# Attention sinks of the last batch moved into the preceding key block, with late fetches for the displaced keys

## The chip, the core and the metric

The kernel runs on one core of a Trainium2 chip. The metric is the device time of one execution in microseconds (us). Six executions of the kernel before took 226.69 to 228.21 us, median 227.55.

## What is computed

Attention with a sliding window and four sinks, then layer normalisation and a two-layer product with a residual:

```python
keep = is_sink | in_window          # first 4 keys, or 0 <= q - k < 128
scores = np.where(keep, scale * q @ k.T, -1e9)
a = exp(scores - max); a = a / a.sum(-1)
x = a @ v                           # 4 batches, 8 heads, 768 rows, head width 64
xn = (x - mu) / sqrt(var + 1e-6) * g_ln
out = x + relu(xn @ w_ch1) @ w_ch2  # 512 -> 2048 -> 512
```

Inputs and output are fp32. The products are made in bf16.

## The kernel before, in words

The 4 x 768 rows are cut into 24 blocks of 128 rows, six to a batch (`b, r = divmod(t, 6)`). A block sees its own keys and those of the block ahead of it. For r = 0 and 1 that holds the sinks as well. For r >= 2 the four sink keys of the batch get products of their own.

For each block: load q, k and v (lines 267, 272 and 275, on the GpSimd queue, POOL); transpose q and k (on PE for the first eight blocks, line 347; by DMA from the sync queue SP for the others, line 369); scores `ps` (line 406, PE) and, for r >= 2, sink scores `pk` (line 413, PE); exponentials on ACT (lines 435 and 482); masks on the vector engine DVE (line 444); the products with the values into `po` (sinks at line 496, own and preceding keys at lines 501 and 504, PE); normalisation with row sums (lines 514 and 517, DVE); centring (lines 526 and 529, DVE); variance (lines 537 and 538, DVE); transpose of the centred block `xc` to `xnt` (line 559 on PE for the first eight blocks, line 565 by DMA from SP for the others).

The sink keys of a batch are copied once from its first block into `ks` (line 454, DVE). The sink values are spread over partitions by two small products `pv` (line 466, PE) and masked (line 472, DVE) into `vs`.

Four blocks make a group, so there are six groups. `m1` multiplies a group by w_ch1 in 16 steps (line 603, PE), each followed by a relu on ACT or DVE (lines 619 and 617). `m2` multiplies by w_ch2, four steps for each block (line 638, PE), followed by the output step on DVE (line 650) and a store on SP (line 659). One step of either is four matmuls of 512 columns. The inverse deviation of a group is a power on POOL (line 548), fed by a small DVE step (line 546); it shares POOL's queue with the loads.

The order on every engine's queue is made when the program is built. `Planner` (lines 15 to 126) places tasks one by one: the task whose inputs, buffers and engine are free first, by costs and delays written next to each task, then by a priority. The engines themselves run their queues strictly in order and wait on semaphores. Scores of later blocks are held back by a pace: block t waits for step 8(t-4)-16 of the products (lines 698 to 701). Buffers are rings with a number of slots each (`RINGS`, line 166): `pa` are four PSUM banks, `xn` the `xnt` buffers, `h1` the buffers after the relu, `qk` the transposed q and k. In the opening, PE is given filler matmuls (`warm`, line 181, and `w0`, line 314), as many as the planned gap in time has room for.

Of the kernel before, what the change touches and what calls it, by code (L numbers as in the profile page):

```python
# [7 lines left out]
FP32 = mybir.dt.float32  # L8
BF16 = mybir.dt.bfloat16
I32 = mybir.dt.int32  # L10
# [4 lines left out]
class Planner:  # L15
# [16 lines left out]
    def run(self, free, warm_until):  # L32
# [14 lines left out]
        ends = {}  # L47
        dma_free = free["DMA"]
        order = []
        queued = []  # L50
        while ready:
# [37 lines left out]
            if e == "PE":  # L89
                gaps[i] = start - free[e] if start < warm_until else 0.0  # L90
            free[e] = start + cost
            end = start + cost + (self.LAG[e] if t["lag"] is None else t["lag"])
            ends[i] = start + cost
            if t["land"] is not None:
                dma_free = max(dma_free, start + 1.5) + t["land"]
                end = dma_free + (0.6 if t["lag"] is None else t["lag"])
                if t["desc"]:
                    queued.append((dma_free, t["desc"]))
            done[i] = (e if t["land"] is None else None, start + cost, end)
# [13 lines left out]

    @staticmethod
    def room(queued, desc, ring=4096):

        for at, d in reversed(queued):
            desc += d
            if desc > ring:
                return at  # L120
        return 0.0

    def emit(self, order):
        for i, e, slots in order:
            self.gap = self.gaps.get(i, 0.0)
            self.tasks[i]["emit"](e, *slots)
# [3 lines left out]
def kernel(  # L130
# [34 lines left out]
    LDN, QKN = 4, 5  # L165
    RINGS = dict(pa=4, ps=2, ld=LDN, qk=QKN, ks=2, vs=2, e=8, es=3, xc=4, xn=4, h1=32, ot=4)
    plan = Planner(RINGS)
# [13 lines left out]
    def warm(bank_):  # L181

        for _ in range(int(plan.gap * WARM / .056)):
            nc.tensor.matmul(bank_, lhsT=ident, rhs=ident, start=True, stop=True, skip_group_check=True)
# [20 lines left out]
    blk_h = consts.tile([128, 4], BF16, name="blk_h")  # L205
    ks_t = [consts.tile([128, 2, 4, 32], BF16, name=f"ks_{i}") for i in range(2)]
    xt = [consts.tile([128, DM], BF16, name=f"xt_{t}") for t in range(NT)]

# [9 lines left out]
    def make_masks():  # L218
        v_ = nc.vector
        nc.gpsimd.iota(iota_d, pattern=[[1, 128]], base=0, channel_multiplier=-1)  # L220
        nc.gpsimd.iota(iota_h, pattern=[[-32, 4]], base=0, channel_multiplier=1)
        v_.tensor_scalar(ident, iota_d, 0.0, None, op0=ALU.is_equal)
        v_.tensor_scalar(mask_std[:, 0:128], iota_d, 0.0, None, op0=ALU.is_ge)
        v_.tensor_scalar(tmp_h, iota_h, float(NS), None, op0=ALU.is_lt)
        v_.tensor_tensor(mask_zero, mask_std[:, 0:128],
                         tmp_h[:, 0:1].to_broadcast([128, 128]), op=ALU.max)
        v_.tensor_scalar(neg_zero, mask_zero, 1.0, 30000.0, op0=ALU.subtract, op1=ALU.mult)
# [22 lines left out]
    d_q, d_k, d_v = {}, {}, {}  # L250
    last_load = [None]

    def load(fn, land, take=(), desc=1024):
        i = plan.add({"POOL": 0.88}, [], fn, (0,), take=take, land=land, after=last_load[0], desc=desc)
        last_load[0] = i
        return i
# [55 lines left out]

    P = {}
    def w0(e, s):
        b_ = bank(s, "pw")
        for _ in range(WARM0):
            nc.tensor.matmul(b_[:, 0:128], lhsT=zeros, rhs=zeros, start=True, stop=True, skip_group_check=True)
# [3 lines left out]
    def opening():  # L321
        plan.add({"PE": .1}, [], w0, (0, -1, 0), take=[("pa", "w0", 0)])
        D["mb"] = plan.add({"DVE": .45}, [d_q[0]], make_masks_b, (0, 0, 1))
        D["mc"] = plan.add({"DVE": 1.3}, [d_q[0]], make_masks_c, (0, 1, 5))


# [3 lines left out]
    def block(t):  # L330
# [3 lines left out]
        last = r == RB - 1  # L334
        split = t in SPLIT


# [18 lines left out]
        n_s = lambda u: 2 if u in SPLIT_S else 1  # L356
        qk_readers = n_s(t) + (0 if last else n_s(t + 1)) + (1 if r == 0 else 0)
        if split:
# [26 lines left out]
        def sc(halves):  # L385
# [30 lines left out]
            return f  # L416

        s_ = []
        for halves in (((0,), (1,)) if t in SPLIT_S else ((0, 1),)):
            cost = .22 * nkb + .43 * nkb * (t in MPE)  # L420
            sink = r >= 2 and halves[-1] == 1
            x_ = plan.add({"PE": cost * len(halves) / 2 + .15 + SINK * sink},
                          d_c[t] + (d_c[t - 1] if r else []) + ([D["mb"]] if t in MPE and r else [])
                          + ([d_ks[b]] if sink else []), sc(halves),
                          (0, t, 2), take=[("ps", ("ps", t, h), 1) for h in halves]
                          + ([("pa", ("pk", t), 1), ("es", ("es", t), 2)] if sink else []),
                          drop=[("qk", t)] + ([("qk", t - 1)] if r else []) + ([("ks", b)] if sink else []))
            s_ += [x_] * len(halves)
# [3 lines left out]
        for half in range(2):  # L432
            def ex(e, s, half=half):
                E[t, half] = buf("e", s, [128, 2, 2, 2, 128], BF16, "e")
                nc.scalar.activation(E[t, half][:, :, :, 0:nkb, :], P["ps", t, half][:, :, :, 0:nkb, :], AF.Exp, scale=scale)  # L435

            x_ = plan.add({"ACT": 1.02 if r else .59}, [s_[half]], ex, (0, t, 3),
                          take=[("e", ("e", t, half), 1)], drop=[("ps", t, half)])

            def mk(e, half=half):  # L440
                m = (mask_zero, mask_one)[r] if r < 2 else mask_std
                w = 128 * nkb
                ee = E[t, half].rearrange("p a b c d -> p (a b) (c d)")
                nc.vector.tensor_mul(ee[:, :, 0:w], ee[:, :, 0:w], m[:, 0:w].unsqueeze(1).to_broadcast([128, 4, w]))  # L444

            ms.append(x_ if t in MPE else plan.add({"DVE": .68 if r else .4}, [x_], mk, (0, t, 4)))


        if r == 0:
            def mks(e, s):  # L450
                ks_of[b] = ks_t[s]
                for h2 in range(2):
                    rows = slice(64 * h2, 64 * h2 + 64)
                    nc.vector.tensor_copy(ks_of[b][rows, h2], qkT[t][rows, 1, :, 0:32])

            d_ks[b] = plan.add({"DVE": .3}, d_c[t], mks, (0, t + 2, 0), take=[("ks", ("ks", b), 4)],
                               drop=[("qk", t)])
            vs_d = []
            for half in range(2):
                hs = slice(4 * half, 4 * half + 4)  # L460

                def pv_(e, s, *s2, half=half, hs=hs):
                    if s2:
# [4 lines left out]
                pv = plan.add({"PE": .13}, [d_v[t], D["mc"], s_[0]] + vs_d, pv_, (0, t + 2, 0),  # L468
                              take=[("pa", ("pv", b, half), 1)] + ([("vs", ("vs", b), 8)] if half == 0 else []))

# [7 lines left out]

        a_deps = [d_v[t]] + ([d_v[t - 1]] if r else [])
        if r >= 2:  # L480
            def es_(e):
# [6 lines left out]
        for half in range(2):  # L488
            def av(e, s, half=half):
# [3 lines left out]
                ee = E[t, half]  # L493
                if r >= 2:
                    for h2 in range(2):
# [3 lines left out]
                for hh in range(4):  # L499
                    h = 4 * half + hh  # L500
                    nc.tensor.matmul(po[:, hh, :], lhsT=ee[:, h % 2, hh // 2, 0, :], rhs=vn[:, t, h, :],  # L501
                                     start=(r < 2 and hh == 0), stop=(r == 0), skip_group_check=True)
                    if r > 0:
                        nc.tensor.matmul(po[:, hh, :], lhsT=ee[:, h % 2, hh // 2, 1, :], rhs=vn[:, t - 1, h, :],  # L504
                                         start=False, stop=True, skip_group_check=True)

            a = plan.add({"PE": (.12, .25, .37)[min(r, 2)]}, a_deps + [ms[half]], av, (0, t, 5),
                         take=[("pa", ("po", t, half), 1)],
                         drop=[("e", t, half)] + ([("es", t), ("vs", b)] if r >= 2 else []))

            def nm(e, half=half):
                po = P["po", t, half]
                rc = small.tile([128, 4], FP32, name="rc")
                nc.vector.reciprocal(rc, po[:, :, 64])  # L514
# [6 lines left out]

            ns.append(plan.add({"DVE": .60}, [a], nm, (0, t, 6), drop=[("po", t, half)]))

# [9 lines left out]
        def st(e):  # L533
            if ti == 0:
                mvg[g] = small.tile([128, 4, 2], FP32, name="mvg")
            st_ = small.tile([128, 6], FP32, name="st")
            nc.vector.bn_stats(st_, xt[t])  # L537
            nc.vector.bn_aggr(mvg[g][:, ti, :], st_)

        v_ = d_var[t] = plan.add({"DVE": .87}, [l_] + ([d_var[t - 1]] if ti else []), st, (0, t + 6, 7))  # L540
        if ti == len(GROUPS[g]) - 1:
# [40 lines left out]
    quanta = []  # L582
    ks_of = {}


    h1 = {}
# [86 lines left out]
    MPE = set(range(4))  # L673
    W2AT = 6
    SEQ = [x for g in range(NG) for x in ((1, g), (2, g))]
    for t, parts in ((0, "qk"), (1, "qk"), (0, "v"), (2, "qk"), (1, "v"), (3, "qk"), (2, "v"), (3, "v")):
# [14 lines left out]
    for i, (layer, g) in enumerate(SEQ):  # L691
        mark[layer, g] = len(quanta)
        (m1(g, i, SUBS.get(g)) if layer == 1 else m2(g, i))
    pace = []
    for layer, g in SEQ:
# [6 lines left out]
    make_consts()  # L702
    order = plan.run(dict(PE=3.5, DVE=4.6, ACT=2.0, POOL=1.2, SP=1.0, DMA=3.4), WARM_UNTIL)
    plan.emit(order)
# [35 lines left out]
```

## Time and profile before

| | |
|---|---|
| median of six executions | 227.55 us (226.69 to 228.21) |
| the profiled execution | 228.21 us |
| its span in the profile | 226.1 us |
| PE busy | 216.8 us, 96% of the span |
| DVE busy | 134.7 us, 60% |
| ACT busy | 104.1 us, 46% |
| POOL busy | 76.0 us, 34% |
| chain that ended last: PE, DMA, POOL, DVE | 81%, 7%, 5%, 4% |
| granted TensorE clock, mean | 1.00 |

The profile shows one execution. Its page gives busy times, 40 slices of the span (each digit the busy share in tenths), the chain of work that ended last, followed back from the end, and groups of instructions with count, busy time, mean duration, and the idle time ahead of them with what ended it. In the chain in order of time, a line holds the start in us, the length in us, and what ran. A matmul's record lasts longer than its share of PE's time, since matmuls overlap; the chain's pieces show the share. `DMA qkT<-qkn` is a transfer on the chain, from its issue to its landing.

### The profile page before, as it was taken

To read this page: it belongs to the slowest core of one execution; us is meant where nothing else is said; L and a number is where in the kernel's file an instruction comes from. 1 tells how busy PE (TensorE), PEld (TensorE's weight loads), DVE (VectorE), ACT (ScalarE), POOL (GpSimd) and SP (SyncE) were. 2 spreads that over 40 slices of the span, in tenths; PEclk is the share of its full clock that TensorE was granted. 3 is DMA by queue.
4 is the path that set the end of the run, shared out by engine and by line. 5 is a ranking of instruction groups with operands and counts; after the bars stand their busy time and mean duration, and the time that the engine had idled before them with its cause. 6 is when DMAs were issued, how large, how long until landed. Compare 5 with 4: busy or idle time off the path is not lost.

```text
span 226.1 us, 4819 instructions
## 1 busy us (share of the span) xinstructions
PE 216.8 (96%) x1938; PEld 121.9 (54%) x1964; DVE 134.7 (60%) x399; ACT 104.1 (46%) x166; POOL 76.0 (34%) x92
## 2 busy tenths in 40 slices
PE   8998999999799999999999999999999999999993
PEld 7665887655355554554555544554554544444452
DVE  5776988779567989755658673845863722100121
ACT  2486888344168650356660347641266610267000
POOL 7994365592593440950269000010000010000000
PEclk9999999999999999999999999999999999999999
DMA  6999999999999999999999996213121011200112
GB/s 42 142 157 202 183 184 207 168 176 185 152 188 143 147 140 196 153 159 169 138 105 163 140 202 120 47 26 116 49 70 23 3 43 73 93 0 3 46 46 93
DMA packets 108853, 26.52 MB, mean 117 GB/s; under 512 B 101536, under 2 KB 105888, under 8 KB 108832
## 3 DMA queue, kind: packets, MB, share of 16 engines
q0 software_dynamic: 79104, 13.64, 80.3%
q1 hardware_dynamic: 29728, 12.59, 31.7%
q8 instruction: 15, 0.25, 0.5%
q14 instruction: 6, 0.05, 0.1%
HBM read 27.27 MB, written 6.29 MB: 148 GB/s over the span
## 4 chain that ended last, share of the span: by engine, by line
PE 81%; DMA 7%; POOL 5%; DVE 4%; issue 1%; ACT 0%; POOLq 0%; ACTq 0%
PE ph L603 34%; PE pc L638 34%; PE ps L406 5%; DMA qkT<-qkn 4%; DMA w1s<-in_moe_w_ch_dram 3%; PE po L501 2%; PE po L504 2%; POOL qkn L267 2%; POOL qkn L272 2%; PE po L496 2%; POOL vn L275 2%; PE pk L413 1%; DVE w1s L299 1%; PE pt L347 1%; DVE xt L517 1%
## 5 line engine op out<-in xcount | busy, mean ns | idle before, releaser
L603 PE MATMUL ph<-xnt,w1s 128*128 128x512 bf16 (+1 forms) x434 | 88.9, 348 | 1.3 <-DVE w1s L299 0.3
L638 PE MATMUL pc<-w2s,h 128*128 128x512 bf16 (+1 forms) x388 | 87.1, 370 | 1.0 <-issue 0.5
L619 ACT ACTIVATE h<-ph 128x512 bf16<-128x512 f32 (+1 forms) x84 | 45.9, 547 | 53.7 <-PE ph L603 52.0
L603 PEld LDWEIGHTS <-w1s 128*128 128x128 bf16 x448 | 41.5, 98 | 35.7 <-DVE w1s L299 0.9
L638 PEld LDWEIGHTS <-h 128*128 128x128 bf16 x400 | 37.4, 98 | 37.8
L435 ACT ACTIVATE e<-ps 128x1024 bf16<-128x1024 f32 (+1 forms) x48 | 43.7, 954 | 12.9 <-PE ps L406 12.9
L650 DVE SCALAR_TENSOR_TENSOR ot<-pc,rsg,xt 128x512 f32<-128x512 f32 (+1 forms) x25 | 18.2, 726 | 38.4 <-PE pc L638 38.4
L548 POOL TENSOR_TENSOR rsg<-ve,eps_half 128x4 f32<-128x4 f32 x6 | 6.2, 1028 | 79.6 <-DVE ve L546 79.6
L267 POOL DMA_DIRECT2D qkn<-in_q_dram x24 | 21.9, 915 | 18.4 <-DMA qkT<-qkn 15.7
L444 DVE TENSOR_TENSOR e<-e,mask_std 128x1024 bf16<-128x1024 bf16 x28 | 18.9, 684 | 10.9 <-ACT e L435 10.9
L617 DVE TENSOR_SCALAR h<-ph 128x512 bf16<-128x512 f32 (+1 forms) x28 | 15.9, 570 | 14.9 <-PE ph L603 14.9
L272 POOL DMA_DIRECT2D qkn<-in_k_dram x24 | 21.8, 909 | 3.1 <-DMA w1s<-in_moe_w_ch_dram 1.6
L275 POOL DMA_DIRECT2D vn<-in_v_dram x24 | 21.9, 915 | 1.7 <-DMA w1s<-in_moe_w_ch_dram 1.7
L517 DVE SCALAR_TENSOR_TENSOR xt<-po,rc 128x256 bf16<-128x256 f32 x48 | 20.4, 425 | 1.7
L501 PE MATMUL po<-vn,e 128*128 128x65 bf16 x192 | 17.1, 193 | 0.3 <-DMA vn<-in_v_dram 0.3
L537 DVE BATCH_NORM_STATS2 st<-xt 128x6 f32<-128x512 bf16 x24 | 16.4, 685 | 0.0
L406 PE MATMUL ps<-qkT 64*128 64x128 bf16 x352 | 14.7, 218 | 1.6 <-DMA qkT<-qkn 1.3
L406 PEld LDWEIGHTS <-qkT 64*128 64x128 bf16 x352 | 9.9, 94 | 11.3 <-issue 8.1
L482 ACT ACTIVATE es<-pk 128x256 bf16<-128x256 f32 x16 | 6.1, 384 | 20.7 <-PE pk L413 20.7
L501 PEld LDWEIGHTS <-e 128*128 128x128 bf16 x192 | 14.0, 97 | 2.5 <-issue 0.4
L514 DVE RECIPROCAL rc<-po 128x4 f32<-128x4 f32 x48 | 8.6, 178 | 11.4 <-PE po L504 10.3
L504 PE MATMUL po<-vn,e 128*128 128x65 bf16 x160 | 14.9, 193 | 0.0
(66 smaller groups left out, 144.1 us busy)
## 6 DMA issues: line engine op xcount, KB each, us to landing
out_dram<-ot SPq DMA_DIRECT2D x23, 256.0 KB, 3.6
qkn<-in_q_dram POOLq DMA_DIRECT2D x24, 128.0 KB, 7.1
qkn<-in_k_dram POOLq DMA_DIRECT2D x24, 128.0 KB, 7.2
vn<-in_v_dram POOLq DMA_DIRECT2D x24, 128.0 KB, 7.9
w1s<-in_moe_w_ch_dram POOLq DMA_DIRECT2D x4, 512.0 KB, 10.5
w2s<-in_moe_w_ch_dram POOLq DMA_DIRECT2D x4, 512.0 KB, 11.8
qkT<-qkn SPq DMA_TRANSPOSE x16, 7.7
xnt<-xc SPq DMA_TRANSPOSE x16, 5.2
```

Of the source, the lines that this page charges most:

```text
L267: nc.gpsimd.dma_start(qn[t][:, 0], q[b, :, rows, :].rearrange("h p d -> p h d"))
L272: nc.gpsimd.dma_start(qn[t][:, 1], k[b, :, rows, :].rearrange("h p d -> p h d"))
L275: nc.gpsimd.dma_start(vn[:, t, :, 0:64], v[b, :, rows, :].rearrange("h p d -> p h d"))
L406: nc.tensor.matmul(ps[:, h2, hh, kb, :], lhsT=qkT[t - kb][rows, 1, hp, :], rhs=qkT[t][rows, 0, hp, :], start=(hh == 0 and kb == 0 and t no ...
L435: nc.scalar.activation(E[t, half][:, :, :, 0:nkb, :], P["ps", t, half][:, :, :, 0:nkb, :], AF.Exp, scale=scale)
L444: nc.vector.tensor_mul(ee[:, :, 0:w], ee[:, :, 0:w], m[:, 0:w].unsqueeze(1).to_broadcast([128, 4, w]))
L501: nc.tensor.matmul(po[:, hh, :], lhsT=ee[:, h % 2, hh // 2, 0, :], rhs=vn[:, t, h, :], start=(r < 2 and hh == 0), stop=(r == 0), skip_grou ...
L504: nc.tensor.matmul(po[:, hh, :], lhsT=ee[:, h % 2, hh // 2, 1, :], rhs=vn[:, t - 1, h, :], start=False, stop=True, skip_group_check=True)
L517: nc.vector.scalar_tensor_tensor(xt[t][:, 256 * half:256 * half + 256].rearrange("p (h d) -> p h d", h=4), in0=po[:, :, 0:64], scalar=1.0, ...
L603: nc.tensor.matmul(ph, lhsT=w1s[:, j, 128 * ht:128 * (ht + 1)], rhs=xnt[g][:, j, cols], start=(j == 0), stop=(j == NDM - 1))
L619: nc.scalar.activation(o, i, AF.Relu)
L638: nc.tensor.matmul(P["pc", t, cols.start][:, cols], lhsT=h1[g, ht][:, 128 * ti:128 * (ti + 1)], rhs=w2s[:, ht, cols], start=(ht == 0), sto ...
```

## The change

In blocks with r >= 2 of the last batch (`FOLD = 18`: blocks 20 to 23), the sink keys and values are written over rows 0 to 3 of the preceding block (`fold_k`, `fold_v`, DVE), after that block's own use of them. The mask of r = 1, which lets those rows through, is taken for these blocks. `pk`, its exponential, the two sink products of `po` and `pv` are left out there. The overwritten rows 1 to 3 still belong to the window of the block's first three query rows. Their part is computed apart: nine small fetches on SP bring the three queries, keys and values of each of the four blocks to 12 partitions, a chain of 13 DVE steps and one exponential makes the weighted sums, a small DMA spreads them to three partitions, and the normalisation adds them to rows 0 to 2 of `po`. The fetches wait for a memset that waits for product step 112, the first `m1` step of group 3.

The variance may be computed on ACT as well, with a scaled square and its row sum. The ring of `xnt` buffers shrinks from 4 to 2, that of `h1` from 32 to 20. A number of planned costs and delays differ (loads, the opening, the normalisation), and the planned landing of transfers from SP takes the loads under way on POOL into account. The filler matmuls ahead of a planned 7 us count as 0.11 us each and no longer as 0.056. The built program has 32 `pk` matmuls fewer (96), 16 sink products of `po` fewer (48), two `pv` fewer (6), and 54 filler matmuls by `warm` for 66. On ACT stand ten of the 24 variances.

```diff
+    FOLD = 18
-    RINGS = dict(pa=4, ps=2, ld=LDN, qk=QKN, ks=2, vs=2, e=8, es=3, xc=4, xn=4, h1=32, ot=4)
+    RINGS = dict(pa=4, ps=2, ld=LDN, qk=QKN, ks=2, kss=2, vs=2, e=8, es=3, xc=4, xn=2, h1=20, ot=4)
...
-        for _ in range(int(plan.gap * WARM / .056)):
+        for _ in range(int(plan.gap * WARM / (.056 if plan.at > 7.0 else .11))):
...
+        nc.gpsimd.iota(iota_c, pattern=[[4, 3]], base=4, channel_multiplier=-1)
...
+    def corrections(gate):
+        def hold(e):
+            nc.vector.memset(f_in[:, 0, :, 0:1], 0.0)
+            nc.vector.tensor_scalar(mask_c[:, 0, :], iota_c, 0.0, None, op0=ALU.is_gt)
+        h_ = plan.add({"DVE": .3}, [gate], hold, (0, 7, 7))
...
+                def fetch(e, n=n, b=b, i=i):
+                    to = f_in[12 * n + 4 * i:12 * n + 4 * i + 4]
+                    nc.sync.dma_start(to[:, :, 0, :], q[b, :, 256:768, :].rearrange("h (r x) d -> x r h d", x=128)[i])
+                    for at, src in ((1, k), (4, v)):
+                        nc.sync.dma_start(to[:, :, at:at + 3, :].rearrange("r h p d -> r h (p d)"),
...
+        for p in range(3):
+            d = step(.68, fetched + [d] if p else fetched, lambda e, p=p: nc.vector.tensor_mul(fk[:, :, p, :], fk[:, :, p, :], fq))
+            d = step(.65, [d], lambda e, p=p: nc.vector.tensor_reduce(
+                fs[:, :, p:p + 1], fk[:, :, p:p + 1, :], axis=mybir.AxisListType.X, op=ALU.add))
+        d = step(.3, [d], lambda e: nc.scalar.activation(fe, fs, AF.Exp, scale=scale), "ACT")
+        d = step(.2, [d], lambda e: nc.vector.tensor_mul(fe, fe, mask_c.to_broadcast([FR, H, 3])))
+        for p in range(3):
+            d = step(.65, [d], lambda e, p=p: nc.vector.tensor_mul(
+                fv[:, :, p, :], fv[:, :, p, :], fe[:, :, p:p + 1].to_broadcast([FR, H, 64])))
+        d = step(.2, [d], lambda e: nc.vector.tensor_reduce(fc[:, :, 64:65], fe.unsqueeze(2),
+                                                            axis=mybir.AxisListType.X, op=ALU.add))
+        d = step(.65, [d], lambda e: nc.vector.tensor_add(fv[:, :, 0, :], fv[:, :, 0, :], fv[:, :, 1, :]))
+        d = step(.65, [d], lambda e: nc.vector.tensor_add(fc[:, :, 0:64], fv[:, :, 0, :], fv[:, :, 2, :]))
+        def spread(e):
+            for n in range(len(FB)):
+                nc.sync.dma_start(fcb[:, 4 * n:4 * n + 4], fc[12 * n:12 * n + 12])
...
+        if fold:
+            def fold_k(e):
+                nc.vector.tensor_copy(qkT[t - 1][:, 1, :, 0:4], kss_of[b])
+            def fold_v(e):
+                nc.vector.tensor_copy(vn[0:4, t - 1], vn[0:4, t - r])
...
-            sink = r >= 2 and halves[-1] == 1
+            sink = r >= 2 and not fold and halves[-1] == 1
...
+                if fold:
+                    nc.vector.tensor_add(po[0:3], po[0:3], fcb[:, 4 * FB.index(b) + r - 2, 4 * half:4 * half + 4, :])
...
+                root = 1.0 / float(DM) ** 0.5
+                st_ = small.tile([128, 1], FP32, name="nb")
+                nc.scalar.mul(st_, sums[t][:, 2:3], -root)
+                nc.scalar.activation(junk, xt[t], AF.Square, bias=st_, scale=root, accum_out=mvg[g][:, ti, 1:2])
...
-        v_ = d_var[t] = plan.add({"DVE": .87}, [l_] + ([d_var[t - 1]] if ti else []), st, (0, t + 6, 7))
+        v_ = d_var[t] = plan.add({"DVE": .87, "ACT": 1.1}, [l_] + ([d_var[t - 1]] if ti else []), st, (0, t + 6, 7))
...
-    order = plan.run(dict(PE=3.5, DVE=4.6, ACT=2.0, POOL=1.2, SP=1.0, DMA=3.4), WARM_UNTIL)
+    order = plan.run(dict(PE=1.0, DVE=4.6, ACT=2.0, POOL=1.2, SP=1.0, DMA=3.4), WARM_UNTIL)
```

## The prediction, made before the run

> **What bounds the kernel now.** I read the page first (busy shares, the 40 slices, the chain), then the windows, then the chain in order of time, then the rows of the vector, scalar, GpSimd and sync engines where the change touches them.
>
> ```profile
> PE 216.8 (96%) x1938; PEld 121.9 (54%) x1964; DVE 134.7 (60%) x399; ACT 104.1 (46%) x166; POOL 76.0 (34%) x92
> PE   8998999999799999999999999999999999999993
> DVE  5776988779567989755658673845863722100121
> DMA  6999999999999999999999996213121011200112
> PE 81%; DMA 7%; POOL 5%; DVE 4%; issue 1%; ACT 0%; POOLq 0%; ACTq 0%
> ```
>
> PE is busy 216.8 of 226.1 us and carries 81% of the chain. The slices show two regimes: up to slice 24 (about 136 us) the DMA engines are also at 9 tenths, after it they are nearly idle. So early work can be held by data, late work only by PE or by what feeds it. The one large wait of PE on data is at 61 us:
>
> ```profile
> 51.09 0.35 PE ps L406 x8
> ...
> 52.16 8.71 DMA qkT<-qkn
> ...
> 60.92 0.62 PE ps L406 x16
> ```
>
> The scores of block 8 need a transpose that was issued at 52.16 and landed 8.71 us later; PE stood idle 1.33 us before them. From there to 210 us PE idles some 1.3 us in all (the windows), in pieces of 0.05 to 0.25. So what is saved behind 61 us is paid out in full; what is saved ahead of it first has to bring that landing forward.
>
> ```profile
> 132.34 0.22 PE pv L466
> ...
> 147.88 0.55 PE ps L406 x16
> 148.43 0.23 PE pk L413 x8
> 148.66 0.16 issue
> ...
> 151.35 0.12 PE po L496 x2
> ```
>
> These are rows of the last batch: sink scores (pk), sink values (po L496) and the gather of sink values (pv, two matmuls) all lie on the chain.
>
> **What the change removes from PE.** Its blocks 20 to 23 lose pk: 0.23, 0.23, 0.22 and 0.23 us on the chain (at 148.43, 156.94, 165.44, 173.95), together 0.91. They lose two L496 pairs each, 8 x 0.12 = 0.96. The batch loses both pv, 0.22. Sum 2.09 us, all behind 61 us. The built order of instructions confirms the counts (pk 128 to 96, L496 64 to 48, pv 8 to 6). Product matmuls and window matmuls are as many as before.
>
> **What it adds to the vector queue (DVE), and what hides it.** The correction of three query rows per block is 11 long instructions (12 partitions, 512 fp32 elements: three products, three sums, three weightings, two additions) and two short ones. No row shows fp32 from SBUF on 12 partitions; these are the nearest:
>
> ```profile
> L444 DVE TENSOR_TENSOR e<-e,mask_std 128x1024 bf16<-128x1024 bf16 x28 | 18.9, 684 | 10.9 <-ACT e L435 10.9
> L650 DVE SCALAR_TENSOR_TENSOR ot<-pc,rsg,xt 128x512 f32<-128x512 f32 x23 | 17.2, 747 | 36.2 <-PE pc L638 36.2
> L537 DVE BATCH_NORM_STATS2 st<-xt 128x6 f32<-128x512 bf16 x24 | 16.4, 685 | 0.0
> ```
>
> L650 has the same width in fp32. Back to back it costs 0.66 (it starts at 151.57, the next at 152.23). I take 0.66 for the long ones; below, 0.43 (the 512-wide bf16 rows); above, 1.05, as no row shows a sum over 64. So 11 x 0.66 + 2 x 0.2 = 7.7 us, and 0.4 for the small exponential on ACT in the middle. In the new order it starts behind the first normalisation of block 19 (ends 143.93 before). Then come that block's second normalisation 0.56, the output step 0.66, the centring 0.51, the copy of sink values 0.35 (0.4 at most, by the 512-wide copy), and block 20's masks 2 x 0.61: 3.3. The masks are ready at 143.9 + 7.7 + 0.4 + 3.3 = 155.3. PE now asks for them ten product steps after block 20's scores: 148.4 + 10 x 0.865 = 157.1. Slack 1.8 us: no cost in the likeliest case.
>
> Behind that each folded normalisation grows by an addition on three partitions, 260 wide: 0.34, the pace of the 260-wide L472 row. It becomes 0.9. Two copies of sinks per block (about 0.2 and 0.35) replace nothing, and four variance steps (0.9 each) move to ACT. Laid out by these paces, block 21's masks come 0.3 us ahead of PE, block 22's 0.4, block 23's about level. I put 0.2 us of waits there (0 to 1.0).
>
> ```profile
> 140.00:150.00 10.00, 9.79 (x91) 5.01 (x88) 4.64 (x14) 7.13 (x12) 1.03 (x1) 1.00 0.21 41
> 150.00:160.00 10.00, 9.95 (x91) 5.13 (x90) 6.51 (x16) 3.15 (x5) 0.00 (x0) 1.00 0.21 66
> 160.00:168.40 8.40, 8.29 (x77) 4.23 (x76) 5.79 (x16) 2.82 (x4) 0.00 (x0) 1.00 0.28 80
> ```
>
> In each window the busy times stand in the order PE, PEld, DVE, ACT, POOL. DVE was at 46 to 69% and rises to over 80%; ACT has room for the variance, a 512-wide activation of about 0.6 and a small one, four times, less four es of 0.38 that go.
>
> **Queues that the nine fetches pass.** They stand on SP behind the transpose of block 22 (132.41, held until block 18's scores) and one store. The memset ahead of them waits for the first step of group 3 on PE, 132.0; DVE has nothing ready then but that step's own output. Nine issues at 0.33 to 0.53 (store rows) end by 139.5; with 2.2 us to landing (stores' median) they are there at 141.7, and DVE asks at 143.9. Behind them on SP wait the transposes xnt of block 18 (needed at 164) and qkT of block 23 (140.42 anyway, held by block 19's scores). The small store of the corrections goes out at about 152.5, and delays the transpose of block 19 to 154; at 5.2 us to landing it beats 162. Zero, with 2 to 4 us of cover each.
>
> **Buffers.** Group product buffers 32 to 20 and xnt buffers 4 to 2: a group's first product already stands behind the last product of the group before on PE; zero. Variance on ACT in earlier batches: off the chain; zero.
>
> **The opening.** One more iota on POOL between the first two loads: 0.08 (the gap that iota_h takes, 2.59 to 2.67). The loads never run dry from there on, so I count 0.1 on the landing at 61. Other reordering around 20 us lets PE do block 2's output transpose and half of block 3 while w1s is scaled; before, PE waited there (0.32, 0.22, 0.20 and part of a 1.16 us row that holds 0.43 of work). That lead of 0.3 to 1.0 us should be lost again at 61 us: the keys of block 8 were issued only at 44.28, when a w2s piece landed, and take 7.2. I count nothing.
>
> The Trainium skill speaks against one edit here. TensorE: Matmul & The Clock Gate, Part 1, says the array runs at half rate until some 3.4 us of activity and falls back after an idle window as long; the change cuts filler matmuls ahead of 8 us from 36 to 11. The row: the first 34 take 3.81 us, 112 ns each, later ones 56, while the granted clock reads 1.00 throughout. By the rule a fallback would double about 1.6 us of work; but the gaps opened are some 0.9, 0.4 and 0.4 us, short of its window, and fillers and idle time ahead of 20 us cover 1.6. Zero.
>
> **POOL's order** changes where it matters to DMA:
>
> ```profile
> 58.91 1.03 POOL L548 TENSOR_TENSOR rsg<-ve,eps_half 128x4 f32<-128x4 f32 x1 [6.35 <-DVE ve L546]
> 59.91 0.93 POOL L272 DMA_DIRECT2D qkn<-in_k_dram  x1
> ```
>
> Before, block 11's keys sat behind this 6.35 us wait. Now they and its values go ahead of it, so about 53 us, into the queue that competes with the transposes of blocks 8 to 10. The skill's DMA: Bandwidth & Descriptors, Queues, rings and completion order, says that a DMA engine takes turns between queues packet by packet. By that, two loads at 0.88 us of issue each could delay block 8's transpose by up to 1.75. The row reads otherwise: 8.71 us is what the backlog of some eight loads at about 1 us takes to clear, against 3.0 for the quickest transpose, as if it waited for what stood ahead; later loads then cost it nothing. I take 0, and keep 1.75. Blocks 9 to 11 are now scored one or two steps earlier, block 9 at about 65.5 and block 10 at 69.2. The loads of blocks 13 and 14 reuse the buffers that these transposes read, and were issued at 64.30 and 66.90, so the transposes had landed by then; block 11's now leaves earlier. No wait there.
>
> **Sum.** 226.1 - 2.09 + 0.1 + 0.2 = 224.3 span; with the 2.1 us around it, 226.4 against the profiled 228.21. That execution is the slowest of six, 0.66 above the median, so I move the difference, -1.8, to the median: 227.55 - 1.8 = **225.7**.
>
> **Rivals.**
> - Likeliest, as summed: 225.7, own range 225.0 to 226.6. Chance 0.58.
> - The saving turns into a wait between 53 and 83 us: loads moved ahead delay transposes, by turns. For: the DMA engines are full, block 8 is already late. Against: the row above. Price 1.75: 227.5. Chance 0.17, nearly all of it within 0.3%.
> - Slower: the vector queue falls behind in batch 3. For: it is in order, its slack is 1.8 and then 0.3 us, and no row prices a sum over 64. Long instructions of 1.05 us put block 20's masks 11 x 0.39 = 4.3 later, 2.5 beyond the slack; growing normalisations then add some 0.6 at blocks 21 and 22: 225.7 + 3.1 = 228.8. It decides from 2.5 us of such waits, so from about 1.0 us an instruction, or if the fetches land after 148. Against: L650 and L537. Chance 0.12.
> - Faster still: the lead of the opening brings forward block 1's output, whose store stands ahead of the transpose on SP, and the wait of 1.33 us goes: 224.4. Chance 0.13.
>
> That the fold doesn't do what it says is excluded by the counts.
>
> **Chances.** A measurement of this kernel can tell about 0.3%, 0.68 us, from no change: 226.87 to 228.23 is the same. Faster 0.57 + 0.02 + 0.13 = 0.72; same 0.16; slower 0.12. The range leaves out the slower rival and small tails: 224.3 to 227.5.
>
> **What would show it.** PE busy down by about 2 us and no pk in batch 3; the wait for block 8's transpose still above 1 us at about 61; group 3 starting within 0.3 us of 131.15; block 20's value matmuls ten steps behind its scores without idle time; long corrections near 0.66. It is wrong if PE waits for masks or sink copies between 155 and 176, or if block 8's scores move by over half a microsecond either way.

## The result, and the profile after

The changed kernel took 226.4 us (median of 31 runs, 223.9 to 228.5) against 227.37 of the kernel before (68 runs, 225.98 to 228.86). The ratio is 0.9932 [0.9915, 0.9949]: 1.55 us faster (1.2 to 1.9), where the prediction said 1.8 and a median of 225.7. The ratio leaves out nine slow executions of the changed kernel, more than 1.5% above its fastest; by the medians of all runs the gain is 1.0 us. The profiled execution took 225.75 us, with a span of 224.0 against 226.1.

From the page of the changed kernel, the lines that answer to those of before:

```profile
PE 213.8 (95%) x1877; PEld 120.4 (54%) x1902; DVE 139.4 (62%) x413; ACT 109.0 (49%) x187; POOL 76.1 (34%) x93
PE   8799999999699999999999999999999999999993
DVE  4687987789559896657548565797897832100121
DMA  7999999999999995999999997205212021200112
PE 88%; DMA 6%; POOL 2%; issue 1%; DVE 1%; POOLq 0%
```

PE is still the chain, with 3.0 us less of work: 2.1 in the last batch, the rest mostly fillers ahead of 8 us. The 6 in the eleventh slice (56 to 61.6 us) is the wait for block 8's transpose. The chain in order of time, there and in the last batch:

```profile
51.28 9.72 DMA qkT<-qkn
...
131.23 0.86 PE ph L717 x4
132.09 0.33 PE ps L487 x8
132.42 2.70 PE ph L717 x12
```

Around the wait, the queue of SP and PE (a bracket gives the idle time and what ended it):

```profile
46.88 4.28 SPq L773 DMA_DIRECT2D out_dram<-ot  x2
51.28 6.78 SPq L450 DMA_TRANSPOSE qkT<-qkn  x2
...
58.49 0.39 PE L673 MATMUL px<-ident,xc 128*128 128x128 bf16 x4
61.05 0.62 PE L487 MATMUL ps<-qkT 64*128 64x128 bf16 x16 [2.18 <-DMA qkT<-qkn]
...
61.83 2.76 PE L717 MATMUL ph<-xnt,w1s 128*128 128x512 bf16 x11
```

and SP of the kernel before:

```profile
46.75 5.23 SPq L659 DMA_DIRECT2D out_dram<-ot  x2
52.16 1.60 SPq L369 DMA_TRANSPOSE qkT<-qkn  x1
```

The transpose was issued 0.88 us earlier than before (52.16), took 1.01 us longer (8.71), and landed at the same time: block 8's scores start at 61.05, before at 60.92. The last `pk` stands at 124.1 and the last sink product of `po` at 128.2, so none is left in the last batch. From the start of block 8's scores to the end of the span it was 226.1 - 60.92 = 165.2 us; now it is 224.0 - 61.05 = 162.95. This measure, "the segment", is used below, since it is free of what happens ahead of 61 us. It fell by 2.2 us.

What the segment does not hold is the time outside the profiled span. The time less the span has a median of 2.11 us in the executions of the kernel before that ran beside the experiments, and of 1.79 in those of the changed kernel; every kernel made from the changed one lies at 1.75 to 1.81. So 0.3 us of the gain lies outside the span; no run says why.

DVE in the last batch of the changed kernel, in order of time:

```profile
143.79 0.68 DVE L386 TENSOR_TENSOR f_in<-f_in 12x512 f32<-12x512 f32 x1
144.50 0.68 DVE L387 TENSOR_REDUCE fs<-f_in 12x8 f32<-12x512 f32 x1
...
153.02 1.27 DVE L536 TENSOR_TENSOR e<-e,mask_one 128x1024 bf16<-128x1024 bf16 x2
...
157.32 0.42 DVE L620 TENSOR_TENSOR po<-po,fcb 3x260 f32<-3x260 f32 x1 [1.93 <-PE po L607]
```

The corrections run from 143.79 to 151.66, block 20's masks are ready at 154.3, and PE asks for them at 157.0. In the last line it is DVE that waits for PE. The windows of the last batch (busy PE, PEld, DVE, ACT, POOL, then granted clock, DMA share, GB/s):

```profile
140.00:150.00 10.00, 9.89 (x81) 4.88 (x78) 8.63 (x20) 7.75 (x12) 0.00 (x0) 1.00 0.16 28
150.00:160.00 10.00, 9.84 (x74) 4.99 (x74) 7.67 (x22) 3.08 (x6) 1.03 (x1) 1.00 0.37 70
160.00:168.40 8.40, 8.35 (x73) 4.27 (x73) 7.67 (x23) 5.25 (x10) 0.00 (x0) 1.00 0.32 92
```

DVE rose from 4.64, 6.51 and 5.79 us to 8.63, 7.67 and 7.67, and PE lost nothing by it.

POOL of the changed kernel around the wait:

```profile
51.05 0.91 POOL L302 DMA_DIRECT2D qkn<-in_k_dram  x1
51.92 0.92 POOL L305 DMA_DIRECT2D vn<-in_v_dram  x1
61.54 0.88 POOL L297 DMA_DIRECT2D qkn<-in_q_dram  x1 [8.70 <-DMA qkT<-qkn]
62.43 1.05 POOL L662 TENSOR_TENSOR rsg<-ve,eps_half 128x4 f32<-128x4 f32 x1
```

Block 11's k and v are issued at 51.05 and 51.92; before it was 59.91 and 60.83, behind the power. This is the row that the explanation comes back to.

### The profile page after: what moved, and what is told of

Read it like the earlier page. It is cut to its first block, busy times and chain, and to the rows that moved or that the text cites. A ratio compares the mean times of both kernels' runs of the same rounds, so it can differ in the third digit from the quotient of the medians.

```text
span 224.0 us, 4744 instructions
## 1 busy us (share of the span) xinstructions
PE 213.8 (95%) x1877; PEld 120.4 (54%) x1902; DVE 139.4 (62%) x413; ACT 109.0 (49%) x187; POOL 76.1 (34%) x93
## 4 chain that ended last, share of the span: by engine, by line
PE 88%; DMA 6%; POOL 2%; issue 1%; DVE 1%; POOLq 0%
PE ph L717 37%; PE pc L752 34%; PE ps L487 5%; DMA qkT<-qkn 4%; PE po L604 3%; DMA vn<-in_v_dram 2%; PE po L607 2%; PE po L599 1%; PE pk L494 1%; PE pt L428 1%; PE ps L478 1%; POOL qkn L297 1%; PE px L673 1%; POOL qkn L302 1%; PE po L196 1%
## 5 line engine op out<-in xcount | busy, mean ns | idle before, releaser
L717 PE MATMUL ph<-xnt,w1s 128*128 128x512 bf16 (+1 forms) x435 | 88.2, 348 | 0.6
L752 PE MATMUL pc<-w2s,h 128*128 128x512 bf16 (+1 forms) x388 | 86.0, 370 | 0.9 <-issue 0.5
L733 ACT ACTIVATE h<-ph 128x512 bf16<-128x512 f32 (+1 forms) x81 | 44.3, 548 | 48.5 <-PE ph L717 47.2
L717 PEld LDWEIGHTS <-w1s 128*128 128x128 bf16 x448 | 41.4, 98 | 34.3
L731 DVE TENSOR_SCALAR h<-ph 128x512 bf16<-128x512 f32 (+1 forms) x31 | 17.8, 576 | 13.5 <-PE ph L717 13.4
L604 PE MATMUL po<-vn,e 128*128 128x65 bf16 x192 | 16.8, 193 | 0.3 <-DMA vn<-in_v_dram 0.3
L536 DVE TENSOR_TENSOR e<-e,mask_std 128x1024 bf16<-128x1024 bf16 x20 | 13.6, 686 | 5.1 <-ACT e L527 4.9
L487 PEld LDWEIGHTS <-qkT 64*128 64x128 bf16 x352 | 9.9, 94 | 11.5 <-issue 7.6
L604 PEld LDWEIGHTS <-e 128*128 128x128 bf16 x192 | 14.0, 97 | 3.1 <-issue 0.4
L607 PE MATMUL po<-vn,e 128*128 128x65 bf16 x160 | 14.7, 193 | 0.0
L607 PEld LDWEIGHTS <-e 128*128 128x128 bf16 x160 | 11.0, 97 | 1.4
L637 DVE TENSOR_SCALAR xc<-xt,sums 128x512 bf16<-128x512 bf16 x24 | 10.5, 436 | 0.8
```

What stands on the lines that cost most here:

```text
L487: nc.tensor.matmul(ps[:, h2, hh, kb, :], lhsT=qkT[t - kb][rows, 1, hp, :], rhs=qkT[t][rows, 0, hp, :], start=(hh == 0 and kb == 0 and t no ...
L717: nc.tensor.matmul(ph, lhsT=w1s[:, j, 128 * ht:128 * (ht + 1)], rhs=xnt[g][:, j, cols], start=(j == 0), stop=(j == NDM - 1))
L733: nc.scalar.activation(o, i, AF.Relu)
L752: nc.tensor.matmul(P["pc", t, cols.start][:, cols], lhsT=h1[g, ht][:, 128 * ti:128 * (ti + 1)], rhs=w2s[:, ht, cols], start=(ht == 0), sto ...
```

## The experiments

Ratios are to the kernel before, run beside each kernel on the same chip. The edits are on the changed kernel unless it says otherwise, and show their main lines. An execution whose mean granted clock is below 0.996 is said to have a dip; every execution of the kernel before beside these runs reads 0.997 or more.

**Without the fold.** Everything else of the change is kept.

```diff
-    FOLD = 18
+    FOLD = 24
...
-    corrections(quanta[GATE])
```

> The changed kernel with the fold taken out (sinks of the last batch computed as in the other batches, no corrections), everything else of the change kept. Theory (the PE work taken out of batch 3 is the whole gain): the 2.1 us come back, span 226.1 and a time equal to the kernel before within 0.5 us, with block 8's scores still starting near 61.0 us. Rival (the new plan, costs and buffers gain or lose something of their own): span below 225.3 or above 226.8.

Measured: 228.06 us, ratio 1.0044 [1.0017, 1.0072]. The span was 224.7 and block 8's scores started at 59.61, so the segment is 165.1, that of the kernel before. The fold is worth 2.1 us by the segment and 2.5 by the ratios (0.0112 of 227). But the remainder of the change is no zero: it costs about 1 us, and still 0.5 in the seven executions without a dip (227.54 against 227.02). The rival's sign came too (a span below 225.3), but it points the wrong way: this one execution is short because block 8's scores started early, at 59.61 for the expected 61.0.

**The correction chain made longer.** Four more products of [12, 512] in fp32 follow the exponential, or eight in a second kernel; no order changes.

```diff
+            for _ in range(4):
+                nc.vector.tensor_mul(fc[:, :, 0:64], fk[:, :, 2, :], fq)
```

> Four more long vector instructions (12 partitions, 512 fp32) inside the correction chain, at an unchanged order of all instructions: 4 x 0.65 = 2.6 us. In the changed kernel block 20's masks are done at 154.3 and PE uses them at 157.0, 2.7 us of slack. Theory (the chain is covered): PE waits at most 0.3 us at block 20, span 224.0 to 224.6. Rival (the vector queue has no room behind the chain): 0.8 to 1.5 us lost, span 224.8 to 225.5.

> Eight more such instructions, 5.2 us, order unchanged. Theory: 2.7 us are covered and 2.5 us show as a wait of PE at block 20's value products, with up to 0.8 us more at blocks 21 and 22: span 226.5 to 227.3, so the whole gain of the fold is gone. Rival (there is more cover, since the engines drift apart and later work catches up): span below 225.5.

Measured: with four, 225.85 us, 0.9947 [0.9917, 0.9977], segment 163.3: 0.3 us more than without. PE does not wait for masks; the span of 224.8 falls to the rival only because block 8's scores started late, at 61.54. With eight, 231.1 us, 1.0193 [1.0155, 1.0231]: the cover is used up, and the span of 228.8 is longer than either theory had it. The waits of PE and then three windows of the kernel with eight:

```profile
PE po L609 <- DVE e L541: 2.3, 1, 2.3
```

```profile
148.00:158.00 10.00, 9.68 (x58) 4.29 (x56) 9.65 (x20) 2.38 (x4) 0.00 (x0) 1.00 0.01 2
158.00:161.00 3.00, 0.96 (x16) 0.80 (x16) 2.96 (x7) 1.02 (x3) 0.00 (x0) 0.85 0.37 116
161.00:165.00 4.00, 4.00 (x30) 1.98 (x28) 3.31 (x14) 2.12 (x3) 1.03 (x1) 0.68 0.27 83
```

Eight products at 0.65 are 5.2 us, less 2.7 of slack 2.5: PE's wait was 2.3. The loss is larger than the wait, 4.2 us by the segment (167.1), because behind it the granted clock falls (last column but two: 1.00, 0.85, 0.68) and block 21's scores take 1.12 us where they take 0.62. The slower rival's mechanism is real; the changed kernel stands 2.7 us away from it.

**The fillers of the opening as before** (22, 9 and 9 ahead of 8 us for 3, 4 and 4; the kernel before has 18, 9 and 9, so 36 and not 40). Two numbers of the planner go back as well, so that the order on PE stays.

```diff
-        for _ in range(int(plan.gap * WARM / (.056 if plan.at > 7.0 else .11))):
+        for _ in range(int(plan.gap * WARM / (.056))):
```

> The filler matmuls ahead of 8 us as many as in the kernel before (40 against 11), nothing else moved on PE. Theory (fillers cover nothing that sets the end; PE waits for block 8's transpose at 61 us in any case): span 224.0 within 0.3, block 8's scores within 0.2 us of 61.05. Rival (fewer fillers cost clock in the opening, or free PE for earlier work): block 8's scores or the span move by over 0.5 us.

Measured: 226.39 us, 0.9978 [0.9947, 1.0009]; segment 162.9. No gain. The span was 223.3 and block 8's scores started at 60.40, each over 0.5 us off, as the rival had it; but the starts in these profiles scatter by more than that without a change of fillers (59.61 without the fold, 61.54 with the longer chain). Five of its ten executions had a mean granted clock below 0.996 and were 1.5 us longer than the others (227.07 against 225.52), and 15 of 32 of the changed kernel were 1.9 longer (227.33 against 225.44). I suspected PE's longer wait at 61 us (2.18 us for 1.33).

**Fillers in the wait at 61 us**, with and without the fold.

```diff
+                    for _ in range(32 if t == 8 and half == 0 else 0):
+                        nc.tensor.matmul(ps.rearrange("p a b c d -> p (a b c d)")[:, 0:128],
+                                         lhsT=ident, rhs=ident, start=True, stop=True, skip_group_check=True)
```

> The changed kernel with 32 more filler matmuls (ident by ident, 128x128) placed directly ahead of block 8's scores, where PE waits 2.18 us in the profile; at 0.056 each they fill 1.8 us of that wait and add nothing but up to 0.3 us in executions whose wait is shorter. Theory of the idle gap: the changed kernel's timed executions with a mean granted clock of 0.984 to 0.992 (14 of 32, about 1.7 us longer than those at 0.998 or above) come from PE standing still there; with the gap filled the clock is 0.996 or above in nearly all executions, the span stays about 224.0, the median comes down to about 225.3 and the ratio to the kernel before to about 0.989. Rival, the dips come from the opening or from elsewhere: about four executions in ten stay at 0.984 to 0.992 and the ratio stays 0.993 to 0.995.

> The kernel without the folded sinks (all six late blocks take the sink strip on PE, no corrections), with the same 32 fillers ahead of block 8's scores. Leaves nothing out of what is computed. If the fold is worth 2.1 us in every execution, this is 2.1 us (0.9%) above the kernel with the fold and the same fillers, in time and in span counted from block 8's scores. If the idle gap makes the dips of the granted clock, this one loses them too and comes within 0.3 us of the kernel before (ratio 0.998 to 1.002), where without fillers it was 1.0044; if they come from elsewhere it stays at 1.003 to 1.006.

Measured: 225.83 us, 0.9933 [0.9909, 0.9958], and 228.02 us, 1.0027 [1.0003, 1.0051]. Three of 11 and four of 12 executions still read 0.989 to 0.992. As the cause of all dips, the gap at 61 us falls; whether it made some of them, so few executions cannot tell. The pair gives the fold once more, on one chip: 2.2 us, segments 162.9 and 165.1.

**Block 8's q and k transposed on PE**, and **the variance on DVE alone**.

```diff
+    DTQ = set(range(9, NT))
...
-        elif t in DTR:
+        elif t in DTQ:
```

```diff
-        v_ = d_var[t] = plan.add({"DVE": .87, "ACT": 1.1}, [l_] + ([d_var[t - 1]] if ti else []), st, (0, t + 6, 7))
+        v_ = d_var[t] = plan.add({"DVE": .87}, [l_] + ([d_var[t - 1]] if ti else []), st, (0, t + 6, 7))
```

> The changed kernel with block 8's q and k transposed on PE (8 transposes, about 0.46 us of PE, and two evictions) in place of the DMA transpose whose landing ends PE's 2.18 us wait at 61 us. If that one landing holds back the rest, PE goes on from 58.9 us, pays 0.46 and the median falls by about 1.5 us. If it is the whole queue of transposes that is late, the wait moves to block 9's, and the gain is 0.8 us or less, with a wait of 1 us or more on PE for block 9's qkT.

> The changed kernel with the variance back on DVE alone. The prediction put the ACT share of the variance at nothing for the time. If DVE's slack in batch 3 (2.7 us ahead of block 20's PV products in the changed kernel's profile) and earlier carries it, the ratio to the kernel before stays 0.990 to 0.996 and the end of the span counted from block 8's scores stays within 0.4 us of 162.95. If the sharing is what pays for the corrections' room on DVE, it comes out 0.5 to 1.5 us slower than the changed kernel, with waits of PE on masks or evictions in batch 3.

In both the planner makes another order, so more differs than the line edited.

Measured: 225.17 us, 0.9902 [0.9873, 0.993], which by the ratios is 0.7 us better than the changed kernel, within the intervals, with 0.26 us of the wait gone over to block 9's transpose; and 224.64 us, 0.9876 [0.9843, 0.991], four executions each. The second is faster than the changed kernel, by intervals that just miss each other, which neither theory had said. Its segment is 222.1 - 60.01 = 162.1, 0.86 us shorter, and its order shows why: four matmuls of L717 stand ahead of block 8's scores instead of behind them.

```profile
58.43 1.03 PE L717 MATMUL ph<-xnt,w1s 128*128 128x512 bf16 x4
60.01 0.62 PE L487 MATMUL ps<-qkT 64*128 64x128 bf16 x16 [0.55 <-DMA qkT<-qkn]
```

They fill the wait. That the order gains and the choice of the engine by itself nothing is argued from this; no run changes one without the other.

The profile of the kernel with the PE transpose has a mean clock of 0.992, and its rows and windows show where it is lost:

```profile
6.32 0.40 PE L428 MATMUL pt<-ident,qkn 128*128 128x128 bf16 x4 [0.69 <-DMA qkn<-in_k_dram]
...
8.19 0.55 PE L428 MATMUL pt<-ident,qkn 128*128 128x128 bf16 x4 [1.25 <-DMA qkn<-in_q_dram]
```

```profile
4.00:8.00 4.00, 2.19 (x27) 1.69 (x24) 3.14 (x10) 0.59 (x1) 4.00 (x5) 1.00 1.61 103
8.00:12.00 4.00, 3.81 (x33) 2.45 (x34) 0.98 (x5) 1.78 (x3) 4.00 (x6) 0.57 2.37 151
```

PE waited 0.69 and 1.25 us for k and q of the opening, was busy 2.19 of 4 us, and then ran at 0.57 (0.50 in every half microsecond from 8.5 to 11.5). The changed kernel, in the same windows:

```profile
4.00:8.00 4.00, 2.93 (x32) 2.43 (x30) 2.78 (x10) 0.59 (x1) 4.00 (x5) 1.00 1.70 109
8.00:12.00 4.00, 3.60 (x46) 1.82 (x43) 1.95 (x9) 2.13 (x4) 4.00 (x6) 1.00 2.36 150
```

In the kernel before:

```profile
4.00:8.00 4.00, 3.87 (x58) 3.42 (x56) 3.06 (x11) 0.59 (x1) 4.00 (x6) 1.00 1.76 112
```

The other two profiles that show the dip there (0.59 and 0.57) had 2.39 and 2.19 us of work in the first window, the others of the changed order 2.65 or more. The wait at 61 us doesn't absorb such a dip: in the two of these three profiles that transpose block 8 by DMA, this transpose is issued at 52.11 and 52.13, otherwise at 50.65 to 51.28 (and at 52.38 and 52.69 where PE had waited 0.7 and 1.3 us for ACT). It stands on SP behind two stores of outputs, and these come from PE.

**POOL's order undone, and done alone.** The power goes ahead of block 11's k and v, and of the loads behind them, again in the changed kernel (the lines that hold back v and q like k are not shown); and in the kernel before, nothing is changed but that they go ahead of it.

```diff
+            if e is not None and (late or t == 11):
+                late.append(lambda: lk(None))
+                return
             nc.gpsimd.dma_start(qn[t][:, 1], k[b, :, rows, :].rearrange("h p d -> p h d"))
...
                 nc.gpsimd.tensor_tensor(rsg[g][:, 0:n], ve[:, 0:n], eps_half[:, 0:n], op=ALU.pow)
+                for f in late:
+                    f()
```

In the kernel before:

```diff
             nc.gpsimd.dma_start(vn[:, t, :, 0:64], v[b, :, rows, :].rearrange("h p d -> p h d"))
+            if t == 11:
+                for f in late:
+                    f()
...
+                late.append(pw_) if g == 1 else pw_()
```

> The changed kernel with one thing undone: on POOL's queue the rsg of line 662 goes ahead of block 11's k and v and block 12's q again, as in the kernel before, so that those loads are issued at about 59 to 62 us instead of 51 to 53. The order on PE, DVE, ACT and SP is the changed kernel's. Theory: the two 128 KB loads, sent alongside, make block 8's DMA transpose land later (9.1 to 9.7 us in six profiles of the changed order against 8.7 before); then it lands 0.5 to 1 us earlier here, and the median comes down by as much, to a ratio of 0.988 to 0.991 to the kernel before. Rival, the backlog clears either way as the prediction took it: the ratio stays at 0.992 to 0.995 and the transpose's wait above 9.0 us.

> The kernel before with the same one thing changed the other way: block 11's k and v go ahead of the rsg on POOL, every other engine's order untouched. Theory of the loads alongside: 0.5 to 1 us slower than the kernel before, with block 8's scores starting that much later and the segment behind them unchanged at 165.2. Rival: within 0.3 us of the kernel before (ratio 0.9985 to 1.0015).

Measured: undone, 224.33 us (6 executions), 0.988 [0.9852, 0.9908], which lies just clear of the changed kernel's interval; done alone, 228.43 us (8 executions), 1.0087 [1.0048, 1.0125]. Both times went the way the theory said, and further: by the ratios 1.2 us less and 2.0 us more (1.5 by the medians). Left to the executions without a dip, the kernel before rises by 1.3 us (226.92 to 228.26), and the changed one falls by 0.8 (225.44 to 224.2, less the 0.45 us by which the kernel before was quicker on this chip, 226.92 for 227.37). The transpose in the chain of the kernel with the order undone, and PE's row behind it:

```profile
50.65 8.81 DMA qkT<-qkn
59.50 0.62 PE L498 MATMUL ps<-qkT 64*128 64x128 bf16 x16 [1.27 <-DMA qkT<-qkn]
```

and its POOL:

```profile
50.24 0.90 POOL L302 DMA_DIRECT2D qkn<-in_q_dram  x1
59.23 1.03 POOL L673 TENSOR_TENSOR rsg<-ve,eps_half 128x4 f32<-128x4 f32 x1 [8.09 <-DVE ve L671]
60.23 0.93 POOL L310 DMA_DIRECT2D qkn<-in_k_dram  x1
61.15 0.89 POOL L316 DMA_DIRECT2D vn<-in_v_dram  x1
```

The loads stand behind the power again, the transpose takes 8.81 us, as before (8.71), and block 8's scores start at 59.50; the segment is 162.9. The same rows of the other kernel:

```profile
51.37 9.15 DMA qkT<-qkn
60.57 0.62 PE L411 MATMUL ps<-qkT 64*128 64x128 bf16 x16 [1.78 <-DMA qkT<-qkn]
```

With the loads ahead, the transpose of the kernel before takes 9.15 us (8.71), and PE waits 1.78 us for it (1.33). Block 8's scores did not start later in this profile, as the theory had it, but at 60.57 (60.92), since PE came to the wait at 58.8 and not at 59.6; the segment is 165.1, as expected. The profiled execution itself is no slower (span 225.7), since it is the quickest of its eight and that of before is among the slowest; the price stands in the times.

**Both better versions joined:** the variance on DVE with POOL's order undone, and with the PE transpose.

> The changed kernel with the variance on DVE alone, by which the plan puts four L717 matmuls (0.86 us) ahead of block 8's scores, and with block 11's k and v behind the rsg as before. If both effects are real they add: 0.9 us from the matmuls that now fill the wait and up to 1 us from the earlier landing, less whatever of the wait is then no longer there (it was 0.55 us in the profile with the variance on DVE, so at most that much is left to gain in that execution): median 223.8 to 224.6. If only the matmuls matter: 224.6 as with the variance on DVE alone.

> The changed kernel with the variance on DVE alone and block 8's q and k transposed on PE: no DMA transpose is left ahead of block 8's scores, and the next one, block 9's, was asked for at 62.0 and landed at 62.25 in the profile of the PE transpose alone. If DVE carries both (the two evictions and the variance), 0.3 to 0.8 us faster than either change alone, 224.0 to 224.7; if the wait comes back at block 9's transpose because PE gets there sooner, no faster than 225.2, with a wait of 0.8 us or more on block 9's qkT.

Measured: 224.74 us, 0.9904 [0.9869, 0.9939], and 225.71 us, 0.992 [0.9892, 0.9949]. Neither adds anything. In the first PE doesn't wait for block 8's transpose at all (scores at 60.49), so an earlier landing has nothing more to give; the expected 223.8 to 224.6 was missed. In the second, PE waits for outputs and normalisations on DVE instead (0.4 and 0.3 us). Its wait for block 9's transpose, which I had named as the other way, didn't show.

## Why the prediction came out as it did

**PE's work in the last batch: right.** 2.09 us was said; 2.1 to 2.2 us by segments (162.95 against 165.1 and 165.2), 2.2 by the pair on one chip.

**The correction chain: right, with slack to spare.** The long instructions run at 0.65 (0.66 said), masks are ready at 154.3 (155.3), PE asks at 157.0 (157.1). The folded normalisation grew to 1.02 (0.9). The 0.2 us of waits did not come: outside the wait at 61 us and the opening, the trace of the changed kernel has no wait of PE above 0.2 us. The runs with a longer chain confirm the model: 2.6 us more cost 0.3, 5.2 us more are 2.3 us of waiting.

**The nine fetches: right.** They were issued by 136.6 (139.5 said), the spread went out at 151.76 and the transpose of block 19 at 153.23 (152.5 and 154); nothing waited.

**The variance on ACT: right against the kernel before.** I put it at zero, and without the fold the segments are equal (165.1 and 165.2). What I did not see is that another order would put 0.86 us of PE's work into the wait at 61 us; neither the kernel before nor the changed one has it there.

**The opening: the reason given was wrong, the size is open.** "That lead of 0.3 to 1.0 us should be lost again at 61 us." In the two profiles it wasn't: the stores ahead of the transpose came forward, and with them its issue, by 0.88 us, as the rival "faster still" had it, to which I gave 0.13. But this issue moves as much between executions. In the kernel before with POOL's order changed, where nothing that it stands behind differs, it is at 51.37, and in the profiles of the changed order at 50.65 to 52.69. In the times 0 to 0.7 us is left for the lead (below). With POOL's order undone the time is that of the rival (224.33, said 224.4), but partly by luck: the wait that was to go is still 1.27 us, and 0.3 us comes from outside the span.

**POOL's order: wrong, and the largest miss.** "I take 0, and keep 1.75." It costs 0.8 to 2.0 us, by two kernels that change it in opposite directions. I had read the 8.71 us as the time of a backlog in order, which later loads couldn't touch. The Trainium skill, DMA: Bandwidth & Descriptors, Queues, rings and completion order, says that an engine takes turns between queues by packets. The price agrees with that and with my 1.75; that turns are the mechanism no run isolates. What the runs show is the price and, in the profiles, 8.7 and 8.8 us for the transpose with the loads behind and 9.1 to 9.7 with them ahead, but for one of 8.70. That the whole price passes through this one transpose is not shown: some 0.5 us, between the medians, is what the profiles have of it.

**The clock: too kind.** Fewer fillers and two waits in the opening were put at zero, as the gaps (0.9, 0.4, 0.4 us) fell short of the window that the skill states (TensorE: Matmul & The Clock Gate, Part 1: some 3.4 us). Here the measurement differs from the page: gaps of 0.69 and 1.25 us in one such stretch went ahead of a clock of 0.57. About half of the changed kernel's executions have a dip, 1.9 us each. That all of them lie in the opening is argued from three profiles, not shown; that bringing the fillers back didn't remove them stays open.

So the fold carries the gain, and that the total came so near is partly luck: terms that I had at nothing nearly cancel. Without a dip the time fell by 1.9 us (225.44 against 227.37). The fold gives -2.2, POOL's order +0.8 to +1.3, and the time outside the span, which I had left at 2.1 us, -0.3, so that by difference -0.2 to -0.7 is left for the lead and the rest. (The same sum over the kernel without the fold, +0.5 without dips, leaves 0 to -0.5.) The dips then take back 0.4 of the 1.9 us in the ratio, and 1.0 in the medians of all runs.

## What to carry over

When the order of loads changes on a queue that competes with a transfer PE waits for, price it, and not at zero because they come later: here it cost 0.8 to 2.0 us. A lead ahead of a data wait need not be lost if the transfer's issue itself hangs on that lead, so follow the issuing queue back to what it stands behind. And where a wait of PE remains, look which work the planner could put into it: an order with four matmuls moved ahead gained about as much as any edit of the transfers.

## What the runs showed of the hardware that was not expected

Fp32 products on 12 partitions, 512 wide, and sums of 64 over the same tile cost the same on DVE: 0.67 and 0.68 us each, 0.65 in a row. A stretch of TensorE at a granted clock of 0.50 followed less than 2 us of idle time, in two pieces, and in the last batch a lower clock (0.68 over 4 us) a single wait of 2.3 us; the wait of 2.18 us at 61 us in the changed kernel's profile was followed by 1.00.
